# First attention chunk in more steps, a fifth exp buffer, weight loads on another queue, and a different filler pace

## Chip, cores and metric

The kernel runs on one core of one Trainium2 chip. The metric is device time in microseconds (us) of one execution; the median of several runs is quoted. All runs below are of the state that the measurement calls fast. The *granted clock* is the share of TensorE's full clock that the chip allowed, 1.00 at most.

## The reference

Two layers, each of attention and an MLP, with a residual and a layer norm (without gain) ahead of both. Everything is bfloat16.

```python
x = A_x                                  # [1, 2048, 512]
for _ in range(2):
    x = x + attention(layernorm(x), A_wqkv, A_wo)   # 32 heads of 16 columns
    x = x + relu(layernorm(x) @ B_w1) @ B_w2        # 512 -> 1792 -> 512
# attention: softmax(q k^T / 4) v per head, then @ wo
```

The exponentials are 2 layers x 32 heads x 2048 x 2048 elements, and they set the pace.

## The kernel before

A Python scheduler emits the whole program slot by slot. A **slot** is three blocks of scores (each 128 keys x 512 queries of one head) in three PSUM banks, and one ScalarE instruction that exponentiates them. In some slots ("short") the third block goes to a polynomial on VectorE, two such blocks making a **pair**. All other TensorE work, the **filler** (projections, MLP, transposes for layer norm), is put between the slots, and has one PSUM bank, `ps_f`, that VectorE must empty each time. Keys come in 16 row blocks, heads in four groups `T`, queries in four chunks `j`. While chunk 0 of layer 0 runs, the keys and values of the other chunks are still being made, so its runs are cut in two, with partial sums kept between:

```python
for l in range(2):
    early = range(TPC if l == 0 else NKB - TPC)      # TPC = 4, NKB = 16
    late = range(len(early), NKB)
    sums = acc0 if l == 0 else acc
    for T in range(4):
        add_run(l, 0, T, early, store=sums)
    for T in range(4):
        add_run(l, 0, T, late, load=sums)
    # ... cut: the other chunks
```

The order in which the filler for it is queued, and its pace in matmuls per slot:

```python
for j in range(1, NQS):
    # ... cut: layer norm of chunk j
    work.append(k_group(0, j, 0))
    work.extend(ln_groups(tag, xnT[j], 0, TPC, []))
    work.append(k_group(0, 0, j))
    work.extend(v_group(0, kb) for kb in range(j * TPC, (j + 1) * TPC))
for T in range(1, 4):
    work.extend(k_group(0, T, j) for j in range(1, NQS))

pace = (
    3.0 if first["short"] and not first["l"] else max(todo / max(rest + (AHEAD if first['l'] and first['j'] < NQS - 1 else -6.0), 6.0), 0.5)
)
```

If a slot needs something that is not made yet, the scheduler emits all that it depends on at once (`run_until`). The weight blocks of the MLP are loaded four ahead, from GpSimd's queue, which also holds the broadcast of the softmax sums:

```python
def load_w1(n):
    # ... cut
    nc.gpsimd.dma_start(out=w1buf[n % NW1][:], in_=B_w1[...])

def recip():                                        # softmax normalisation
    nc.vector.reciprocal(out=c, in_=c)
    nc.sync.dma_start(out=sums, in_=c)              # u<-c
    nc.gpsimd.dma_start(out=r[:, 0:width], in_=...) # r<-u, waits for u<-c
```

The matmuls of values with exponentials ("value matmuls") follow one or two slots later, and polynomial pairs are allowed from a certain point on:

```python
while len(pend) > held and len(musts) == copies:
    emit_pv()
# ... cut
elif len(pairs) < 2 and ("k", mine["l"], 0 if mine["l"] else 3, NQS - 1) in made:
```

The softmax here doesn't subtract the row's maximum and nothing guards it: scores larger than these inputs give would overflow.

## Time and profile before

| | before |
|---|---|
| median of three runs | 1783.71 us |
| span of the profiled run | 1781.0 us |
| ScalarE busy | 97% |
| full / short slots | 1071 / 294 |
| first and last exponential start | 16.9 / 1749.7 us |
| mean granted TensorE clock | 0.994 |

The lines are in the prediction.

### The profile page before, as it was taken

The page shows a single profiled execution, that of the slowest core. Times are in us where ns is not written, and L with a number is a line of the kernel's source. Part 1 is how long each engine was busy: PE and PEld are TensorE (multiplying, and loading weights), DVE is VectorE, ACT ScalarE, POOL GpSimd, SP SyncE. Part 2 cuts the span into 40 slices and gives each one's busy share as a digit, 9 for nine tenths or more (in the row PEclk, how much of TensorE's full clock was granted, in tenths as well). Part 3 has the DMA queues.
Part 4 walks back from the last instruction along what each step waited for, and adds up shares of the span by engine and source line. Part 5 has one row for each costly group of instructions (what it writes and reads, how often), then busy time and mean ns, then how long its engine had stood idle before and what let it go on. Part 6 is the DMA issues. An engine that isn't in the chain of part 4 may idle for free.

```text
span 1781.0 us, 35078 instructions
## 1 busy us (share of the span) xinstructions
PE 1643.0 (92%) x15322; PEld 517.8 (29%) x15322; DVE 1349.6 (76%) x2051; ACT 1724.1 (97%) x1386; POOL 149.4 (8%) x231
## 2 busy tenths in 40 slices
PE   8898889999999999999999998999999999999988
PEld 2222222222222222222222222222222222444444
DVE  7438778899899888898732244988888888898784
ACT  7979999999999999999999999999999999999994
POOL 1000000110001000110002000011000110002013
PEclk9989999999999999999999999999999999999999
DMA  4000100110011000110001002101100110102112
GB/s 148 1 7 14 19 15 10 40 26 13 9 22 38 16 13 14 23 40 14 9 9 39 1 3 37 19 17 37 25 20 11 28 35 19 23 14 47 26 31 66
DMA packets 50457, 44.54 MB, mean 25 GB/s; under 512 B 34304, under 2 KB 42240, under 8 KB 50304
## 3 DMA queue, kind: packets, MB, share of 16 engines
q0 software_dynamic: 23296, 33.15, 8.4%
q1 hardware_dynamic: 25664, 7.85, 1.8%
q8 instruction: 119, 1.95, 0.5%
q10 hardware_dynamic: 1344, 1.31, 0.2%
q14 instruction: 34, 0.28, 0.1%
HBM read 22.54 MB, written 2.10 MB: 14 GB/s over the span
## 4 chain that ended last, share of the span: by engine, by line
ACT 87%; PE 8%; DVE 3%; issue 2%; DMA 1%; POOL 0%; POOLq 0%
ACT e L1119 87%; PE ps_s L1110 2%; PE ps_f L403 2%; PE ps_o L806 2%; PE ps_s L1182 1%; DMA w<-in_B_w_dram 0%; DMA c<-u 0%; DVE di L852 0%; DVE dy L883 0%; DVE vaug L552 0%; DVE stats L432 0%; DVE de L883 0%; PE ps_f L1182 0%; PE ps_s L951 0%; DMA x<-in_A_x_dram 0%
## 5 line engine op out<-in xcount | busy, mean ns | idle before, releaser
L1119 ACT ACTIVATE e<-ps_s 128x1536 bf16<-128x1536 f32 (+1 forms) x1366 | 1713.7, 1472 | 20.1 <-PE ps_s L1110 19.3
L1110 PE MATMUL ps_s<-q,ktp 32*128 32x512 bf16 (+1 forms) x8114 | 769.0, 358 | 100.6 <-ACT e L1119 88.5
L806 PE MATMUL ps_o<-e,vaug 128*32 128x512 bf16 (+1 forms) x4270 | 429.5, 364 | 11.7 <-DVE u L744 6.2
L1110 PEld LDWEIGHTS <-ktp 32*128 32x128 bf16 x8114 | 235.8, 92 | 625.5 <-issue 523.0
L852 DVE TENSOR_SCALAR di<-ps_s 128x512 int32<-128x512 f32 x294 | 202.0, 687 | 94.8 <-PE ps_s L1110 92.7
L806 PEld LDWEIGHTS <-vaug 128*32 128x32 bf16 x5284 | 140.5, 94 | 295.3 <-issue 274.1
L883 DVE SCALAR_TENSOR_TENSOR dy<-dm 128x1024 f32<-128x1024 f32 x147 | 179.7, 1222 | 3.9
L883 DVE SCALAR_TENSOR_TENSOR dy<-dy,dm 128x1024 f32<-128x1024 f32 x147 | 178.6, 1215 | 2.7
L883 DVE SCALAR_TENSOR_TENSOR de<-dy,di 128x1024 bf16<-128x1024 f32 x147 | 178.2, 1212 | 1.8
L767 POOL DMA_DIRECT2D r<-u x70 | 51.0, 729 | 1260.6 <-DMA u<-c 373.7
L403 PE MATMUL ps_f<-xn2T,w 128*128 128x512 bf16 (+1 forms) x448 | 129.2, 374 | 5.1 <-DMA w<-in_B_w_dram 2.7
L601 POOL DMA_DIRECT2D w<-in_B_w_dram x126 | 96.2, 764 | 361.7 <-PE ps_f L403 340.8
L403 PE MATMUL ps_f<-w,ht 128*128 128x512 bf16 x392 | 117.8, 384 | 0.0
L616 DVE TENSOR_SCALAR ht<-ps_f 128x512 bf16<-128x512 f32 x105 | 72.2, 687 | 56.5 <-PE ps_f L403 56.2
L806 PE MATMUL ps_o<-de,vaug 128*32 128x512 bf16 (+1 forms) x676 | 104.7, 357 | 0.9
L877 DVE TENSOR_SCALAR dm<-di 128x1024 int32<-128x1024 int32 x147 | 103.2, 702 | 1.2
L877 DVE TENSOR_SCALAR di<-di 128x1024 int32<-128x1024 int32 x147 | 102.1, 695 | 2.2
L403 PE MATMUL ps_f<-xnT,wqkv 128*128 128x512 bf16 (+1 forms) x296 | 88.2, 376 | 2.8 <-DVE ktp L524 1.1
L403 PE MATMUL ps_f<-wo,ot 128*128 128x512 bf16 x240 | 74.0, 385 | 1.1 <-DVE x L587 1.1
L564 DVE TENSOR_SCALAR q<-ps_f,qmask 128x512 bf16<-128x512 f32 (+1 forms) x86 | 56.7, 692 | 15.0 <-PE ps_f L403 14.7
L757 DVE SCALAR_TENSOR_TENSOR ot<-u,mask,r 128x512 bf16<-128x512 f32 (+2 forms) x74 | 49.6, 671 | 23.8 <-DMA r<-u 23.6
L806 PE MATMUL ps_o<-di,vaug 128*32 128x512 bf16 (+1 forms) x338 | 66.1, 365 | 0.3 <-DVE di L877 0.3
(85 smaller groups left out, 561.9 us busy)
## 6 DMA issues: line engine op xcount, KB each, us to landing
w<-in_B_w_dram POOLq DMA_DIRECT2D x126, 128.0 KB, 2.6
r<-u POOLq DMA_DIRECT2D x56, 256.0 KB, 7.1
out_dram<-x SPq DMA_DIRECT2D x16, 128.0 KB
x<-in_A_x_dram SPq DMA_DIRECT2D x14, 128.0 KB
w<-in_B_w_dram SPq DMA_DIRECT2D x1, 1792.0 KB
r<-u POOLq DMA_DIRECT2D x14, 128.0 KB, 4.5
wqkv<-in_A_wqkv_dram ACTq DMA_DIRECT2D x2, 512.0 KB
c<-u SPq DMA_DIRECT2D x56, 8.0 KB
```

The source lines that it names most:

```text
L403: nc.tensor.matmul(out, lhsT, rhs, start=i % k == 0, stop=i % k == k - 1)
L564: return nc.vector.tensor_scalar(out=qbuf[n % 2][e][:, 0:w], in0=b, scalar1=qmask[e][:, 0:1], scalar2=None, op0=ALU.mult,)
L601: nc.gpsimd.dma_start(out=w1buf[n % NW1][:], in_=B_w1[:, ft * P : (ft + 1) * P].rearrange("(c p) f -> p c f", p=P),)
L616: nc.vector.tensor_scalar(out=htp[ft // 2][:, ft % 2 : ft % 2 + number, a : a + w], in0=b.rearrange("p (f q) -> p f q", f=number), scalar1 ...
L757: nc.vector.scalar_tensor_tensor(out=ot[t][:, at_column + a : at_column + a + w], in0=u[:, a : a + w], scalar=mask[e][:, 0:1], in1=r[:, a ...
L767: nc.gpsimd.dma_start(out=r[:, 0:width], in_=bass.AP(tensor=sums.tensor, offset=sums.offset, ap=[list(sums.ap[0]), [0, 32], [1, width]],),)
L806: nc.tensor.matmul(ps_o[32 * g : 32 * g + 32, 0 : sg["w"]], vaug[sg["l"]][kb][:, 4 * sg["T"] + g, 2 * e : 2 * e + 32], rhs, start=g not in ...
L852: first = nc.vector.tensor_scalar(out=di[:, half, :].bitcast(I32), in0=src, scalar1=EXP_BIAS, scalar2=0.0, op0=ALU.add, op1=ALU.max,)
L877: nc.vector.tensor_scalar(out=out[:].bitcast(I32), in0=di[:].bitcast(I32), scalar1=keep, scalar2=put, op0=ALU.bitwise_and, op1=ALU.bitwise_or,
L883: nc.vector.scalar_tensor_tensor(out=out[:], in0=x[:], scalar=c, in1=y[:], op0=ALU.add, op1=ALU.mult)
L1110: nc.tensor.matmul(b[:, a : a + sg["w"]], kt[32 * g : 32 * g + 32, kc : kc + P], qbuf[sg["n"] % 2][sg["e"]][32 * g : 32 * g + 32, 0 : sg[" ...
L1119: ex = nc.scalar.activation(out=eb[:, 0 : place[m]], in_=b[:, 0 : place[m]], func=ACTF.Exp, scale=1.0 / (LOG2E * UNIT),)
```

## The change

Its intent is to keep ScalarE fed: smaller steps in the first chunk, so that no run asks for keys before they are made; value matmuls held back when they would block the scores; weight loads in another queue; filler that need not be finished at a chunk's end.

```diff
-    NE = 4
+    NE = 5
-    AHEAD = 8.0
+    AHEAD = (8.0, 8.0)
+    LATE = 0.0
+    MID = 2
+    FIRST_K = {1: (1, 2, 3), 2: (), 3: ()}
...
-            nc.gpsimd.dma_start(
+            nc.sync.dma_start(
                 out=w1buf[n % NW1][:],
...
+        if l == 0:
+            steps = [(range(4), 0, TPC), (range(MID), TPC, 2 * TPC)]
+            steps += [(range(MID), 2 * TPC, NKB), (range(MID, 4), TPC, NKB)]
+        else:
+            steps = [(range(4), 0, NKB - TPC), (range(4), NKB - TPC, NKB)]
+        for Ts, a, b in steps:
+            for T in Ts:
+                sums = acc if l else acc0
+                add_run(l, 0, T, range(a, b), load=a and sums, store=b < NKB and sums)
...
-                nc.vector.tensor_copy(out=sg["store"], in_=ps_o[:])
+                if sg["load"] is not None:
+                    nc.vector.tensor_add(out=sg["store"], in0=sg["load"], in1=ps_o[:])
+                else:
+                    nc.vector.tensor_copy(out=sg["store"], in_=ps_o[:])
...
-        work.append(k_group(0, j, 0))
+        work.extend(k_group(0, T, 0) for T in FIRST_K[j])
...
+        if j == 1:
+            work.extend(k_group(0, T, 1) for T in range(1, MID))
     for T in range(1, 4):
-        work.extend(k_group(0, T, j) for j in range(1, NQS))
+        work.extend(k_group(0, T, j) for j in range(2 if T < MID else 1, NQS))
...
-   pace: rest + (AHEAD if first['l'] and first['j'] < NQS - 1 else -6.0)
+   pace: rest + (0.0 if first["j"] == NQS - 1 and not first["l"] else AHEAD[first["l"]] if first["j"] < NQS - 1 else -6.0)
...
         while len(pend) > held and len(musts) == copies:
+            start = pe_start("v", at([("po",)], "pe") if ("po",) in made else 0.0)
+            if len(pend) < NE - 1 and start + LATE > exp_end[no] - PE_TO_ACT - 2 * MM - SWITCH:
+                break
             emit_pv()
```

(The two pace lines are cut out of the long expression shown above; cuts are marked by "...".)

More of the change, by code (lines that the diff above doesn't have):

```diff
@@ L694, in add_run @@
                     "l": l, "j": j, "t": 2 * T + e, "e": e, "T": T, "kbs": kbs, "n": n,
-                    "load": load and load[2 * T + e], "store": store and store[2 * T + e],
+                    "load": load[2 * T + e] if load else None,
+                    "store": store[2 * T + e] if store else None,
                     "w": columns(l, j)[2], "begun": set(), "left": 4 * len(kbs), "short": bool(load or store), "early": bool(store), "busy": len(kbs) == TPC,
@@ L700 @@
     for l in range(2):
-        early = range(TPC if l == 0 else NKB - TPC)
-        late = range(len(early), NKB)
-        sums = acc0 if l == 0 else acc
-        for T in range(4):
-            add_run(l, 0, T, early, store=sums)
-        for T in range(4):
-            add_run(l, 0, T, late, load=sums)
+        if l == 0:
[7 more added lines that the diff above has]
+                add_run(l, 0, T, range(a, b), load=a and sums, store=b < NKB and sums)
         for j in range(1, NQS + l):
@@ L1084 @@
         pace = (
-            3.0 if first["short"] and not first["l"] else max(todo / max(rest + (AHEAD if first['l'] and first['j'] < NQS - 1 else -6.0), 6.0), 0.5)
+            3.0 if first["short"] and not first["l"] else max(todo / max(rest + (0.0 if first["j"] == NQS - 1 and not first["l"] else AHEAD[first["l"]] if first["j"] < NQS - 1 else -6.0), 6.0), 0.5)
         )
```

## The prediction

> **What bounds the kernel now.** I read the page first: busy time by engine, then the costliest groups. ScalarE is busy for 97% of the span, nearly all of it in one instruction, the exponential at L1119 (1366 times). A slot, below, is one such instruction with the score matmuls that feed it. I then took that line by shape, because its mean mixes full slots (1536 columns) with short ones (1024 columns, the third block being given to a VectorE polynomial).
>
> ```profile
> PE 1643.0 (92%) x15322; PEld 517.8 (29%) x15322; DVE 1349.6 (76%) x2051; ACT 1724.1 (97%) x1386; POOL 149.4 (8%) x231
> L1119 ACT ACTIVATE e<-ps_s 128x1536 bf16<-128x1536 f32 (+1 forms) x1366 | 1713.7, 1472 | 20.1 <-PE ps_s L1110 19.3
> ...
> L1119 ACT ACTIVATE e<-ps_s 128x1536 bf16<-128x1536 f32 x1071 | 1499.5, 1567 | 17.7 <-PE ps_s L1110 17.0
> L1119 ACT ACTIVATE e<-ps_s 128x1024 bf16<-128x1024 f32 x294 | 331.7, 1129 | 2.4 <-PE ps_s L1110 2.3
> ```
>
> Durations overlap (1366 x 1472 ns is more than the busy 1713.7), so the price of a slot is the distance between starts. The view of the one line in a stretch gives first and last start. From 878.8 to 1070.0 us there are 144 slots, 142 full and 2 short: 191.2 us for 141 full and 2 short intervals. From 299.5 to 499.3 us there are 162 intervals, about 120 full and 42 short. The two together give **1.343 us for a full slot and about 0.926 for a short one**. At these rates 1071 full and 294 short intervals are 1438 + 272 = 1710 us. The first exponential starts at 16.9 and the last at 1749.7, 1733 us apart. So **some 22 us are lost** between them, and the head (17 us) and the tail after the last exponential (31 us) lie outside.
>
> Where are the 22? The same sum, stretch by stretch: start to 106.8 us, 59 full intervals are 79.2 us but took 89.9, **10.7 lost**. 829.0 to 874.8: 1.7 lost. 1068.6 to 1149.8: 2.8. 1499.5 to 1599.4: 0.9. 1718.5 to 1749.7: 18 full and 2 short are 26.0 but took 31.2, **5.2 lost**. The others lose nothing that I can resolve. The waits of ScalarE say the same of the large ones; first the stretch 0 to 120 us, then 1725 to 1740:
>
> ```profile
> ACT e L1119 <- PE ps_s L1110: 10.5, 6, 5.9
> ```
> ```profile
> ACT e L1119 <- PE ps_s L1110: 4.7, 3, 3.4
> ```
>
> The timeline of the first loss shows the cause. The scheduler had put off chunk 2's normalised rows and its K and V until slot 52 could not go on without them:
>
> ```profile
> 87.83 0.38 PE L471 MATMUL ps_f<-ident,xn 128*128 128x128 bf16 x4 [0.46 <-DVE vaug L552]
> ...
> 89.62 0.58 PE L471 MATMUL ps_f<-ident,xn 128*128 128x128 bf16 x4 [0.51 <-DVE xnT L507]
> ...
> 91.82 1.86 PE L403 MATMUL ps_f<-xnT,wqkv 128*128 128x512 bf16 x4 [0.52 <-DVE xnT L507]
> ...
> 95.12 1.45 ACT L1119 ACTIVATE e<-ps_s 128x1536 bf16<-128x1536 f32 x1 [5.91 <-PE ps_s L1110]
> ```
>
> Four groups of transposes each wait for VectorE to empty the one PSUM bank, then come K and four V groups in a row, and ScalarE starves. The table by stretch adds that the granted clock was 0.50 from 90 to 98 us: four K matmuls took 1.86 us there, against 1.02 for the four V matmuls at 103.49 us.
>
> The second loss is in the timeline at the end:
>
> ```profile
> 1726.38 0.68 POOL L767 DMA_DIRECT2D r<-u  x1 [11.61 <-DMA u<-c]
> ...
> 1727.05 3.38 POOL L601 DMA_DIRECT2D w<-in_B_w_dram  x4
> ...
> 1732.26 1.89 PE L403 MATMUL ps_f<-xn2T,w 128*128 128x256 bf16 x8 [2.65 <-DMA w<-in_B_w_dram]
> ...
> 1734.76 1.45 ACT L1119 ACTIVATE e<-ps_s 128x1536 bf16<-128x1536 f32 x1 [3.39 <-PE ps_s L1110]
> ```
>
> GpSimd's queue is in order. Four loads of MLP weights stand behind the broadcast r<-u, which waits for the DMA u<-c; TensorE then waits for weights whose buffers had been free since about 1724.8.
>
> **What the Trainium skill says.** *Perfetto Trace Analysis*, Identifying the Most-Contended Engine: occupancy is a fair measure for Scalar and Vector, not for matmul busy time; so 97% ScalarE is the bound and 92% TensorE is not proof of one. The trace agrees: the stretch from 878.8 ran at the full slot rate with TensorE about 90% busy. *ScalarE: Activation LUTs*, Rules for kernel authors: about 0.3 us plus 0.83 ns an element; here 512 columns are worth 1.343 - 0.926 = 0.417 us, 0.81 ns each, which agrees. *TensorE: Matmul & The Clock Gate*, Part 1: after a window of some 3.4 us with little activity the clock falls to half. The trace agrees: half rate follows 3 us of lone transposes and, in the tail, the 2.65 us wait. *DMA: Bandwidth & Descriptors*, Issuing engines are not separate DMA queues: another issuing engine saves only the sequencer's time. Here an issue takes 0.75 us on GpSimd and 0.54 on SyncE; but the trace shows a second effect, what stands ahead in the queue.
>
> **The change, part by part.** I compared the order of both built programs, counting TensorE's matmuls between neighbouring slots.
>
> (1) *More steps in the first chunk.* Runs of head groups 0 and 1 take row blocks 4 to 7 before they need the rest. That inserts 2 groups x 2 head parities x 4 blocks x 4 heads = 64 blocks, 21 slots, 28 us, before chunk 2 is needed. It costs four more partial sums (4 adds in place on VectorE at about 0.69 us) and two more runs (10 for 8), each with a q group of 4 matmuls and 2 masked copies. VectorE is 27 to 50% busy from 60 to 120 us, so this is hidden. In the new order no slot of the first hundred carries more than 4 transposes or 4 projection matmuls; the 16 transposes and 4 matmuls of slot 52 are gone. At 2 to 4 such matmuls of 0.22 us per slot, with scores and values at about 0.6 us, TensorE stays at or just under 1.343. I take 2 of the 10.7 us as remaining, for short waits on the single filler bank: **-8.7 us**. The lull that lowered the clock goes too, and is in this number.
>
> (2) *Price of it.* The polynomial may start only when the last K group of the chunk is made. The first short slot moves from number 80 to 90, and the program has 145 pairs, not 147: 290 short and 1075 full slots, not 294 and 1071. 4 x 0.417 = **+1.7 us**.
>
> (3) *Weight loads on the sync queue.* In the new order the four late loads stand right behind u<-c, which was issued at 1724.08, not behind r<-u. They can go at about 1724.8 (two) and 1727.6 (two), when their buffers are free. With 2.6 us to landing, the page's median for these loads, the first two are there by about 1728.5 (1724.8, two issues of 0.54, 2.6), and TensorE asks at about 1729.6. The wait and the half clock after it go; I leave 1 of 5.2 us: **-4.2 us**. The 126 issues x 0.75 us that GpSimd no longer makes were not on the path. At the start the loads move behind the other inputs; the head is a chain of VectorE normalisation steps, so nothing is gained there.
>
> (4) *Filler past chunk ends.* In layer 0 the filler had to be done six slots before a chunk's end; now it may run past it. Only the last chunk (829 to 875) loses anything now, 1.7 us, with TensorE packed; the new order has 33, 16, 36 projection matmuls in slots 640 to 699, not 32, 24, 22, so the pack is thinned: **-1.0 us**.
>
> (5) *Five exp buffers and the held value matmuls.* A value matmul that would wait for VectorE to empty the accumulator no longer stands ahead of the next scores. The loss at 1070 to 1150 has such a wait (0.96 us at 1140.3), but the new order is nearly the same there: **-0.5 us**.
>
> Sum: -8.7 + 1.7 - 4.2 - 1.0 - 0.5 = **-12.7 us**; 1783.7 - 12.7 = 1771.0.
>
> **Rivals.** *The loss in the first chunk only moves.* The work to be made there is the same, with two runs more, and TensorE is nearly full over 90 slots instead of 52: every filler group waits for the one bank, 0.5 us or more each. If half of the gain is lost so, the time is 1775. For it: ScalarE lost some already at 57 to 61 us. Against: the waits seen there are under 1 us, and no clump is left. *The sync queue becomes the place to wait.* Loads wait for TensorE, and c<-u and u<-c now stand behind them, so normalisation comes late. For it: DMA c<-u is on the path near 1098 us. Against: there are no weight loads near there, and three buffers of 26 us segments give slack elsewhere. It would cost 1 to 3 us, so 1773. *All losses go:* 22 us less and 1.7 more for the pairs, about 1763; no step above removes the last of each loss. *VectorE gains from a quiet GpSimd:* it is not the bound; nothing.
>
> **Range and chances.** The middle is 1771; the moved loss and the sync queue pull up by up to 6, more thorough removal pulls down by up to 5: 1766 to 1777. A change of 2% is 35.7 us, more than all that is lost, so faster is nearly impossible; a slowdown by as much would need a new wait of 48 us.
>
> **What would show it.** ScalarE's waits in the first 120 us near 2 us, not 10.5, with a clock of 1.0 from 80 to 105; the last 30 slots without a wait on w, the w issues on SyncE; 290 short slots; 31 us still after the last exponential. It would be wrong if ScalarE's start distances rose in the steady stretches, if new waits of scores on the filler bank added up in the first chunk, or if normalisation's DMAs came late behind weight loads.

## The result

The changed kernel took 1769.88 us (four runs, 1769.66 to 1770.96), the kernel before 1784.02 (four runs, 1782.05 to 1784.73). A ratio, here and below, is the mean time of one kernel's fast runs over that of the other's of the same rounds, so not quite the ratio of the medians: **0.9924, interval 0.9907 to 0.9941**. That is within 2%, and inside the range.

The engines' busy times and the costliest group of the changed kernel, in the same form as before:

```profile
PE 1602.8 (91%) x15093; PEld 518.6 (29%) x15289; DVE 1340.4 (76%) x2045; ACT 1724.3 (97%) x1386; POOL 53.5 (3%) x105
...
L1131 ACT ACTIVATE e<-ps_s 128x1536 bf16<-128x1536 f32 (+1 forms) x1366 | 1713.9, 1481 | 5.9 <-PE ps_s L1122 5.1
```

ScalarE is as busy as before; only its idle time before an exponential has fallen, from 20.1 to 5.9 us. GpSimd lost the 126 load issues.

The waits of ScalarE from 0 to 120 us, where there were 10.5 us:

```profile
ACT e L1131 <- PE ps_s L1122: 0.4, 1, 0.4
```

From 1700 to 1745 us the exponential does not occur in that view at all. The table by stretch for 90 to 105 us, first of the kernel before, then of the changed one (columns: stretch, its length, busy us and instruction count of TensorE, its weight loads, VectorE, ScalarE and GpSimd, then the granted clock, DMA share and GB/s):

```profile
90.00:105.00 15.00, 13.26 (x69) 3.51 (x68) 4.06 (x7) 7.04 (x5) 0.00 (x0) 0.67 0.00 1
```
```profile
90.00:105.00 15.00, 13.37 (x115) 4.47 (x113) 6.74 (x12) 15.00 (x13) 0.00 (x0) 1.00 0.00 1
```

TensorE was equally "busy" in both, but at two thirds of the clock and with 69 matmuls instead of 115; ScalarE went from 7 to the full 15 us. Matmul busy time alone would have hidden the loss. And the end, where the weights were late, as a timeline of the changed kernel:

```profile
1716.07 0.54 SPq L776 DMA_DIRECT2D u<-c  x1
...
1716.66 19.68 SPq L604 DMA_DIRECT2D w<-in_B_w_dram  x14
...
1718.37 0.68 POOL L777 DMA_DIRECT2D r<-u  x1 [11.61 <-DMA u<-c]
...
1721.53 1.05 PE L406 MATMUL ps_f<-xn2T,w 128*128 128x256 bf16 x8
```

The loads go out right behind u<-c, 1.7 us before r<-u is issued (before, they came 0.7 us after it), and the eight matmuls that waited 2.65 us now start without a wait and at full clock.

From first to last exponential the changed kernel took 1718.6 us (17.9 to 1736.5), 14.2 us less than before. By the prediction's prices its 1075 full and 290 short slots are 1712.3 us, so some 6 us are lost where it was 22. Its head was 1.0 us and its tail 1.4 us longer in the profiled run. Both go with half clock: from 12 to 14 us the granted clock was 0.50 (the first eight projection matmuls took 2.72 us, not 1.89), and from 1748 to 1750 it was 0.52. In the second profiled run of the changed kernel (e9), without these spells, the head was 16.9 us again and the tail 31.0, and e10, with the loads in the old queue, had a head of 18.3 us with a clock of 0.66 from 10 to 15 us; so it is not the moved loads.

### The profile page after: what moved, and what is told of

It reads as the page before. It is cut to its first block, busy times and chain, and to the rows that moved or that the text cites. A ratio compares the mean times of both kernels' runs of the same rounds, so it can differ in the third digit from the quotient of the medians.

```text
span 1769.2 us, 34798 instructions
## 1 busy us (share of the span) xinstructions
PE 1602.8 (91%) x15093; PEld 518.6 (29%) x15289; DVE 1340.4 (76%) x2045; ACT 1724.3 (97%) x1386; POOL 53.5 (3%) x105
## 4 chain that ended last, share of the span: by engine, by line
ACT 80%; PE 7%; issue 2%; DVE 2%; DMA 0%; ACTq 0%
ACT e L1131 80%; PE ps_s L1122 3%; PE ps_o L816 2%; PE ps_f L406 1%; PE ps_s L1197 1%; DVE di L862 0%; DMA c<-u 0%; PE ps_f L1197 0%; DVE dy L893 0%; DVE q L567 0%; DVE u L754 0%; DVE de L893 0%; DVE u L752 0%; DVE x L647 0%; DVE dm L887 0%
## 5 line engine op out<-in xcount | busy, mean ns | idle before, releaser
L893 DVE SCALAR_TENSOR_TENSOR dy<-dm 128x1024 f32<-128x1024 f32 x145 | 177.2, 1222 | 3.5
L893 DVE SCALAR_TENSOR_TENSOR dy<-dy,dm 128x1024 f32<-128x1024 f32 x145 | 176.2, 1215 | 2.8
L893 DVE SCALAR_TENSOR_TENSOR de<-dy,di 128x1024 bf16<-128x1024 f32 x145 | 175.9, 1213 | 1.8
L406 PE MATMUL ps_f<-xn2T,w 128*128 128x512 bf16 (+1 forms) x390 | 114.0, 368 | 5.6 <-DVE ht L619 2.3
L406 PE MATMUL ps_f<-w,ht 128*128 128x512 bf16 x339 | 105.3, 384 | 4.2 <-issue 3.8
L406 PE MATMUL ps_f<-xnT,wqkv 128*128 128x512 bf16 (+1 forms) x266 | 81.3, 371 | 4.6 <-issue 1.4
L406 PE MATMUL ps_f<-wo,ot 128*128 128x512 bf16 x207 | 65.7, 384 | 2.7 <-issue 2.1
L767 DVE SCALAR_TENSOR_TENSOR ot<-u,mask,r 128x512 bf16<-128x512 f32 (+2 forms) x74 | 49.6, 671 | 14.3 <-DMA r<-u 14.2
L406 PEld LDWEIGHTS <-w 128*128 128x128 bf16 x448 | 33.2, 97 | 81.9 <-issue 73.0
```

The lines of the kernel that those rows point to most:

```text
L406: nc.tensor.matmul(out, lhsT, rhs, start=i % k == 0, stop=i % k == k - 1)
L767: nc.vector.scalar_tensor_tensor(out=ot[t][:, at_column + a : at_column + a + w], in0=u[:, a : a + w], scalar=mask[e][:, 0:1], in1=r[:, a ...
L893: nc.vector.scalar_tensor_tensor(out=out[:], in0=x[:], scalar=c, in1=y[:], op0=ALU.add, op1=ALU.mult)
```

## The experiments

Four kernels carry one part of the change each (e1 to e4), and three the whole but one part (e5, e10, e11). Four add something of mine (e6, e7, e8, e12), and e9 is the changed kernel again. Kernels of one call ran on one chip and shared the runs of the kernel before; e1 to e4 are one call, e5 to e8 the second, e9 to e12 the third. The second call ran on another chip than the other two. All results were correct.

| run | median us | ratio to before | interval |
|---|---|---|---|
| e1 sync queue alone | 1776.62 | 0.9967 | 0.9949 to 0.9985 |
| e2 steps alone | 1774.44 | 0.9954 | 0.9938 to 0.9970 |
| e3 pace alone | 1780.63 | 0.9986 | 0.9971 to 1.0001 |
| e4 hold alone | 1783.30 | 1.0005 | 0.9991 to 1.0019 |
| e5 all but hold | 1769.34 | 0.9926 | 0.9909 to 0.9943 |
| e6 no hold, earlier polynomial | 1770.04 | 0.9930 | 0.9914 to 0.9947 |
| e7 and pairs 20 slots apart | 1769.37 | 0.9933 | 0.9916 to 0.9949 |
| e8 and pairs 10 slots apart | 1776.59 | 0.9971 | 0.9955 to 0.9987 |
| e9 the changed kernel again | 1769.36 | 0.9939 | 0.9924 to 0.9954 |
| e10 all but sync queue | 1774.96 | 0.9965 | 0.9950 to 0.9979 |
| e11 all but pace | 1770.94 | 0.9944 | 0.9930 to 0.9958 |
| e12 hold, earlier polynomial | 1768.56 | 0.9929 | 0.9915 to 0.9943 |

### e1: the loads on the sync queue, alone

```diff
-            nc.gpsimd.dma_start(      # in load_w1
+            nc.sync.dma_start(
```

> The kernel before with the MLP weight loads moved to the sync queue and nothing else. Theory (the loads stood in GpSimd's queue behind the broadcast r<-u): the wait of 2.65 us on w near the end and the half clock after it go, ScalarE's waits between 1710 and 1745 us fall from 4.7 to under 1 us, and the time falls by 4 to 5 us, to about 1779. The 10.5 us in the first chunk stay. Rival (c<-u and u<-c now wait behind weight loads): the normalisation comes late and eats the gain, so the time falls by less than 2 us. Rival (VectorE is faster with a quiet GpSimd): the time falls by more than 6 us and the steady stretches get faster.

The mean fell by 0.33%, 5.9 us, more than the 4 to 5 expected, but the interval runs from 2.7 to 9.1. The trace is clearer: from 1700 to 1745 us the exponential no longer waits, where it had waited 4.7 us, and the loss of that stretch against the slot sum is 5.2 us before and 0.1 here. In the first chunk 9.5 us of waits stay. So the loads' being in GpSimd's queue was the cause. No run separates their place behind r<-u from SyncE's shorter issue (0.37 us for 0.75), but the trace before does in part: the first late load, issued 0.7 us after r<-u, needed 5.2 us to land, where the median is 2.6. Issued at 1724.8 us, when its buffer was free, it would by that median have landed at about 1727.4 even from GpSimd (an estimate), and TensorE asked at 1729.6. The first rival needs c<-u and u<-c to delay something; between 120 and 800 us ScalarE's waits are 0.2 us as before. The second falls too: the steady stretches are as long as before, and VectorE's polynomial steps keep their durations (1222, 1215 and 1212 ns before, 1223, 1216 and 1213 in e1).

### e2: the steps of the first chunk, alone

```diff
-    early, late (two passes over four head groups)
+    steps = [(range(4), 0, TPC), (range(MID), TPC, 2 * TPC)]
+    steps += [(range(MID), 2 * TPC, NKB), (range(MID, 4), TPC, NKB)]
     # with FIRST_K, the order of K groups and the store that adds, as in the change
```

> The kernel before with only the first chunk's attention in more steps and the new order of its K groups; 290 short slots instead of 294. Theory: the clump of 16 transposes and 4 matmuls before slot 53 is the whole loss of the first chunk, so ScalarE's waits up to 120 us fall from 10.5 to about 1 us, the clock stays at 1.0 between 85 and 105 us, and with 1.7 us paid for the four longer slots the time falls by 7 to 9 us, to about 1776. Rival (the loss only moves, the same work meeting the one filler bank over more slots): waits of 4 us or more remain there and the time falls by 3 to 5 us.

The mean fell by 0.46%, 8.2 us. ScalarE's waits up to 120 us are 0.4 us, and the clock is 1.00 in every 5 us from 85 to 105. The rival is out: nothing of the loss came back in that chunk, and from 120 to 800 us the waits are 0.2 us as before. The wait at the end is there as it was, which shows that the parts act in different places:

```profile
1717.99 3.38 POOL L604 DMA_DIRECT2D w<-in_B_w_dram  x4
...
1723.16 1.89 PE L406 MATMUL ps_f<-xn2T,w 128*128 128x256 bf16 x8 [2.61 <-DMA w<-in_B_w_dram]
...
1725.65 1.45 ACT L1131 ACTIVATE e<-ps_s 128x1536 bf16<-128x1536 f32 x1 [3.34 <-PE ps_s L1122]
```

### e3: the filler's pace, alone

```diff
-   rest + (AHEAD if first['l'] and first['j'] < NQS - 1 else -6.0)
+   rest + (0.0 if first["j"] == NQS - 1 and not first["l"] else AHEAD[first["l"]] if first["j"] < NQS - 1 else -6.0)
```

> The kernel before with only the filler's pace changed (in layer 0 it may run past a chunk's end). Theory: only the last chunk of layer 0 (829 to 875 us) loses anything there, 1.7 us, and that goes: the time falls by 1 to 2 us. Rival: the thinning is hidden and nothing changes (within 0.5 us), or work left over at chunk ends collides with the next chunk and it gets slower by 1 us or more.

The ratio 0.9986 has 1 in its interval, so the time does not decide it. The trace has the predicted effect (the loss from 819 to 869 us is 0.5 us instead of 1.7) and a cost that I had not thought of: ScalarE's waits from 120 to 800 us went from 0.2 to 1.1 us. Between these two the gain is too small to be measured alone.

### e4: five buffers and the hold, alone

```diff
-    NE = 4
+    NE = 5
         while len(pend) > held and len(musts) == copies:
+            start = pe_start(...)
+            if len(pend) < NE - 1 and start + LATE > exp_end[no] - PE_TO_ACT - 2 * MM - SWITCH:
+                break
```

> The kernel before with only the fifth exp buffer and the held value matmuls. Theory: the scores no longer stand behind a value matmul that waits for VectorE to empty the accumulator, so the loss of 2.8 us at 1069 to 1150 us shrinks by about 1 us, and the time falls by 0.5 to 1.5 us. Rival: nothing changes (within 0.5 us), because the waits are elsewhere.

The rival: no gain (1.0005). The theory's stretch from 1060 to 1160 us has 2.3 us of waits against 2.0, and new waits appeared elsewhere. ScalarE's waits from 120 to 800 us, 0.2 us before, are here:

```profile
ACT e L1119 <- PE ps_s L1110: 2.3, 5, 0.6
```

### e5: the change without the hold

```diff
-    NE = 5
+    NE = 4
-            start = ...   # the three lines of the hold
```

> The changed kernel with four exp buffers and without the held value matmuls; the rest of the change stays. Theory after the single parts (alone, the held value matmuls raised ScalarE's waits between 120 and 800 us from 0.2 to 2.3 us and took 0.6 from the loss at 1060 to 1145): the part is worth nothing, so the waits between 120 and 800 us fall from 2.8 us to under 1, those at 1060 to 1160 rise from 0.8 to about 1.5, and the time is that of the changed kernel within 2 us (about 1769), rather lower. Rival (the parts need each other: the tighter first chunk is only free of waits because value matmuls are held): waits of 2 us or more come back before 120 us and the time is 2 us or more higher.

At 1769.34 the part is not missed. No wait came back in the first 120 us (0.4 us), so the steps do not need it. From 120 to 800 us the waits fell to 1.8, not under 1. From 1060 to 1160 us they were 3.7 us, more than the 1.5 expected; but that execution had the clock at 0.50 from 1100 to 1105 us.

The traces of e1 to e6, e9 to e12 and the two kernels can tell what the hold does in that stretch. TensorE pauses there in two places of the kernel before: the scores wait for `q` from VectorE, and a value matmul waits for VectorE's copy of the accumulator, the wait that the hold is for.

```profile
1103.79 0.80 PE L1110 MATMUL ps_s<-q,ktp 32*128 32x512 bf16 x7 [0.92 <-DVE q L564]
...
1140.30 0.38 PE L806 MATMUL ps_o<-e,vaug 128*32 128x512 bf16 x1 [0.96 <-DVE u L744]
```

ScalarE alone, first before, then in e1, where TensorE has the same second pause at 1139.19:

```profile
1104.63 37.87 ACT L1119 ACTIVATE e<-ps_s 128x1024 bf16<-128x1024 f32 x31 [0.86 <-PE ps_s L1110]
1143.10 1.45 ACT L1119 ACTIVATE e<-ps_s 128x1536 bf16<-128x1536 f32 x1 [0.60 <-PE ps_s L1110]
1145.13 15.97 ACT L1119 ACTIVATE e<-ps_s 128x1024 bf16<-128x1024 f32 x13 [0.59 <-PE ps_s L1110]
```
```profile
1103.52 57.67 ACT L1119 ACTIVATE e<-ps_s 128x1024 bf16<-128x1024 f32 x47 [0.87 <-PE ps_s L1110]
```

The first pause is in all twelve traces, and ScalarE waits after it. The second is in all six without the hold and in none of the six with it, so the hold does what it was made for; but in e1 ScalarE did not notice it. The rest of the waits follows the clock. Without a spell of half clock in this stretch ScalarE waits 0.8 to 0.9 us (the changed kernel, e1, e12), with one spell 1.7 to 2.3 (eight traces, with and without the hold), with two 3.7 (e5: from 1098.3 and from 1135.8 us).

### A reading across runs: the granted clock

The runs of one kernel differ by up to 10 us. Set beside its mean granted clock, each run falls nearly on a line (the rows for 0.991, 0.993, 0.995 and 0.996, which only the kernel before has, are left out):

| mean clock | kernel before, us | changed kernel, us |
|---|---|---|
| 0.992 | 1785.00 to 1785.97 | none |
| 0.994 | 1782.75 to 1784.26 | none |
| 0.997 | 1779.03 to 1779.33 | none |
| 0.998 | 1779.26 | 1770.96 to 1771.58 |
| 0.999 | 1776.44 | 1769.17 to 1770.04 |
| 1.000 | none | 1768.69 |

A straight line through the 34 runs before with a listed clock falls by 1.24 us for each 0.001, and one through the 9 runs of the changed kernel by 1.40. Half clock appears in spells after a stretch in which TensorE did little. In the profiled runs each spell that ended before the run did lasted 3.41, 6.83 or 10.24 us, and within a run the spells begin whole multiples of 3.41 us apart (before: 89.65, 1140.95 and 1731.46 us, 308 and 173 such steps). Whether a lull is hit differs from run to run: the half clock near 1732 us after the wait for weights was there in the trace before, in e2, e4 and e10, and absent in e3, where the same wait cost 2.4 us in all instead of 4.7. With the clump and the late weights gone, there are fewer lulls to be hit. The mean clock rose from 0.9949 (34 runs) to 0.9988 (9 runs); at 1.24 us for 0.001 that is about 5 of the 12 us between the two means, 1782.1 and 1770.0. This is an estimate from a correlation, not an experiment on the clock. Two cautions for what follows. The listed clock is rounded to 0.001, and so much is worth 1.24 to 1.40 us: a difference of 1 us between a few runs at equal listed clock is a hint, not a result. And a change that removes lulls raises the clock itself, so a comparison at equal clock leaves out part of what it won.

### e9: the changed kernel again

(No edit.)

> The changed kernel again, on the chip of this call, because the runs so far show that a kernel's time follows its mean granted clock (about 1.3 us for 0.001). Theory: the clock of the changed kernel is not fixed at the 0.998 to 0.999 of its first four runs; it varies as for the others, and the time with it, 1769.7 us at 0.999 and about 1.3 us more per 0.001. Rival (the change makes the clock steady): all six runs at 0.998 or more and within 1.5 us of 1770.

Half of my theory fell: the clock of the five runs was 0.998 to 1.000, and all lay between 1768.69 and 1771.58 (the rival's 1.5 us was missed by one run, by 0.08). For these nine runs the change did make the time steadier. The other half held: the time followed the clock, 1768.69 at 1.000 and 1771.22 and 1771.58 at 0.998. The ratio, 0.9939, is nearer to 1 than the first, because the kernel before ran at 1780.36 in this call.

### e10: the change without the sync queue

```diff
-            nc.sync.dma_start(
+            nc.gpsimd.dma_start(
```

> The changed kernel with the MLP weight loads back on GpSimd's queue. Theory (the parts act in different places and add): the wait of about 2.5 to 3.4 us near the end is back, with or without a spell of half clock after it, and nothing else: 3 to 6 us slower than the changed kernel on this chip, about 1774. Rival (another part removes the same wait): within 1.5 us of the changed kernel.

The mean was 1774.6 against 1770.0 for e9, 4.6 us slower, and ScalarE waits 3.5 us near the end again. The rival is out, and 4.6 is the better number for this part, since the runs of these two spread by 2.6 and 2.9 us and those of the kernel before by 8.6 in this call. Part of the 4.6 is half clock: the mean clock was 0.9972 in e10 and 0.9988 in e9.

### e11: the change without the pace

```diff
-   rest + (0.0 if first["j"] == NQS - 1 and not first["l"] else AHEAD[first["l"]] if ...)
+   rest + (AHEAD[1] if first['l'] and first['j'] < NQS - 1 else -6.0)
```

> The changed kernel with the old filler pace. Theory after the single part (at equal clock, 0.997, it stood at 1779.4 against 1779.3 for the kernel before): the thinner filler takes 1 us of waits from 819 to 869 us and gives about as much back between 120 and 800, so at equal clock the time is that of the changed kernel within 1 us. Rival (it is worth the 1 us or more of the prediction): at equal clock more than 1 us slower.

The mean was 1770.8, 0.8 us above e9; at a clock of 0.999 the four runs are 1770.16 to 1771.02 and the five of the changed kernel 1769.17 to 1770.04. The loss from 819 to 869 us is back at 2.0 us (0.2 with the change). The two profiled runs, with one like spell of half clock before the end each (from 1097.6 and 1097.8 us), have spans of 1767.6 (e9) and 1768.4 us. So beside the other parts the pace seems worth about 1 us, on the border between theory and rival; it does not show in the ratios, and the times alone do not settle it.

### e6 and e12: the polynomial earlier in the first chunk

The change paid for its steps with two pairs. Both kernels give them back; e6 is without the hold, e12 with it.

```diff
-   ("k", mine["l"], 0 if mine["l"] else 3, NQS - 1) in made
+   ("k", mine["l"], 0 if mine["l"] else 1, NQS - 1) in made
```

> The changed kernel without the hold, and with the polynomial allowed in the first chunk once K group 1 of the last row block is made, rather than group 3: 294 short slots again, the first at number 76, not 90. Theory (the two lost pairs cost 4 x 0.417 us): 1.7 us less than the changed kernel without the hold, about 1767. Rival (VectorE and the filler bank are too busy there, so the short slots only turn into waits): ScalarE's waits before 170 us rise by 1.5 us or more and the time stays.

> The changed kernel with its hold, and the polynomial allowed in the first chunk once K group 1 of the last row block is made: 294 short slots. Theory: at equal clock 4 x 0.417 = 1.7 us faster than the changed kernel, near 1768.1 at 0.999. Rival: the earlier short slots turn into waits before 170 us and nothing is gained.

e12 has the lowest median of all, 1768.56, but its interval overlaps that of e9. At a clock of 0.999 its four runs (1768.41 to 1768.78) lie 1.0 us below the mean of the changed kernel's five (1769.6), and e6's two (1767.28 and 1767.42) as far below e5's two (1768.30 and 1768.41). So the two pairs seem worth about 1 us rather than 1.7, within the rounding of the clock. In e12, ScalarE's waits from 120 to 800 us are 3.9 where they were 2.8, but that run had a spell of half clock from 518.8 us that the changed kernel's did not. Neither gain is one that the ratios resolve. By median e6 shows nothing, since its clock ran from 0.994 to 0.999.

### e7 and e8: pairs where they were forbidden

In layer 1's first chunk the polynomial waits for the last K group, some 160 slots. Here it may start a pair 20 or 10 slots after the last one.

```diff
+   (... in made or (mine["l"] and no >= last_pair[0] + 20))   # e8: 10
...
                 pair_at = no + 2 if half == 0 else None
+                last_pair[0] = no
```

> As the one before, and in layer 1's first chunk, where the polynomial was forbidden for some 160 slots, one pair may begin at least 20 slots after the last: 302 short slots. Theory (ScalarE is the only bound there, with VectorE about 35% busy): 8 more short slots x 0.417 = 3.3 us less, about 1764. Rival (TensorE, 90% busy there, is the next bound, since a pair's values take three passes): the 190 us stretch keeps its length and the waits take the gain.

> The same with a distance of 10 slots: 310 short slots, but two groups of 8 filler matmuls are now forced at once near slots 831 and 841. Theory: another 8 x 0.417 = 3.3 us less in the stretch, 1 to 2 us given back at the forced groups, so about 1762. Rival (TensorE becomes the bound): no better than the distance of 20, with new waits of 3 us or more between 870 and 1150 us.

Neither theory held in full. e7 gained in its stretch, 146 slots in 189.6 us where the changed kernel had 143 in 190.2, but gave it back in the next: ScalarE's waits from 1060 to 1160 us are 6.3 us. In the timeline TensorE waits for VectorE to add the accumulator to the sums kept before, that addition stands behind a product with r, and the product waits for a DMA:

```profile
1104.34 0.75 DVE L767 SCALAR_TENSOR_TENSOR ot<-u,mask,r 128x512 bf16<-128x512 f32 x1 [4.22 <-DMA r<-u]
...
1106.34 0.59 PE L816 MATMUL ps_o<-e,vaug 128*32 128x512 bf16 x1 [3.93 <-DVE u L752]
...
1107.52 1.45 ACT L1133 ACTIVATE e<-ps_s 128x1536 bf16<-128x1536 f32 x1 [3.72 <-PE ps_s L1124]
```

e8 is clearly worse, with 14.3 us of waits there, and 3.0 from 900 to 1060 us:

```profile
ACT e L1133 <- PE ps_s L1124: 14.3, 8, 3.7
```

The rival had the result right (new waits after 1060 us eat the gain), and only part of the cause: e7's largest wait, 3.72 of 6.3 us, is the normalisation chain and not TensorE's rate. Of e8's three largest, two (3.66 us before 1071.3 and 3.43 before 1090.6) follow a q group and a K group made one after the other, TensorE standing 1.50 us for VectorE's `q` between them; the third (3.02 before 1113.4) is the chain again. What the five smaller ones follow I did not separate.

## Why the prediction was right

**The bound and the loss.** The sum by start distances was the step that carried everything: ScalarE bound, 22 us lost between the exponentials, most of it in two places. The changed kernel has the same busy ScalarE and 14.2 us less between first and last exponential.

**(1) and (2), steps, predicted -8.7 and +1.7.** The mechanism is shown by e2. The size of the first term was off: I left 2 us for waits on the filler bank, and there are none (61 intervals at 1.343 us are 81.9, and 17.9 to 99.6 us took 81.7). So it is -10.7 in the profiled pair, half clock included. One reading of the timeline was off: half clock did not follow 3 us of lone transposes, it began at 89.65 us, 1.8 us after the first of them (87.83). The price of the lost pairs, +1.7, is 290 short slots as counted; e6 and e12, which give the pairs back, seem to have won about 1 us.

**(3), sync queue, predicted -4.2.** Shown by e1 and e10: 5.9 us with a wide interval, and 4.6. I had left 1 us of the stretch's 5.2; 0.1 is left. Where I assumed 0.54 us for an issue on SyncE, the number of another transfer, these loads took 0.37. Two things in the trace before were not in the account: the first late load also took 5.2 us to land, twice the median of 2.6 that the sum used, and half clock began at 1731.46 us, inside the wait and 1.9 us after TensorE's last matmul.

**(4), pace, predicted -1.0.** The trace has it (1.7 us lost before, 0.2 after), e3 did not resolve it, and e11 suggests about 1 us. Not seen in advance was the cost of about 1 us in the steady stretches.

**(5), hold, predicted -0.5.** This step failed. Alone it won nothing and added about 2 us of waits in the steady stretches; without it the rest is as fast (e5). Its two runs at a listed 0.999 are about 1 us below the changed kernel's (1768.30 and 1768.41 against 1769.6), but on another chip and within the rounding of the clock. The pause of 0.96 us that the prediction named goes with the hold, as its mechanism says, but it was not what ScalarE lost there: at full clock that is the wait for `q`, which the hold does not touch, and the rest is half clock that came or did not come (0.9 us in e1, which has no hold; 0.8 and 1.7 in two runs of the changed kernel). Whether the hold makes the clock steadier stays open. The mean is 0.9988 with it over nine runs and 0.9978 over five without (e5), 0.9990 in e12 and 0.9970 in e6, but both without it ran on the other chip; a way would be there, since spells began after either pause and the hold takes one away.

**The rivals.** "The loss only moves" fell with e2. "The sync queue becomes the place to wait" fell with e1 and e10. "VectorE gains from a quiet GpSimd" fell with its unchanged durations.

**What the sum did not have.** The single parts by ratio make -5.9 - 8.2 - 2.5 + 0.9 = -15.7 us; the whole measured -13.5 (0.9924) and -10.9 (0.9939), which intervals of about 3 us either way on each number allow. That the middle was met within 1.1 us is in part luck: the profiled pair shows 2.0 us more won by (1) and 0.9 by (3), and against them 2.6 us of new waits from 120 to 800 us that no term has. The prediction took one trace as if its half clock were the kernel's own. It was a usual run of a spread from 1776 to 1787 us, so the middle was safe, but a base at a clock of 0.999 instead of 0.994 would have shown a loss some 6 us smaller (an estimate, by the line above).

## What to carry to other kernels

When one engine bounds a kernel, price its unit by the distance between starts in a clean stretch, subtract that from every stretch, and look for the cause of each remainder; here two remainders held most of what was to be won. In a queue that works in order, ask what stands ahead of a transfer, not only which engine issues it. When a change is worth a few us and the clock of the runs varies, compare runs of equal granted clock before believing an ordering, unless the change itself removes the pauses that lower it; and leave out a part, not only add it, before calling it useful.

## What the Trainium skill lacked or had wrong

- *ScalarE: Activation LUTs*, Rules for kernel authors: its budget gives the mean duration of one exponential (0.3 us plus 1536 x 0.83 ns is 1.57 us; 1.567 measured), but back to back the starts are 1.343 us apart, 0.22 less. The budget's row says nothing of overlap; an overlap of about 93 ns stands further up on the page (What ACT_TABLE_LOAD costs), and it fits only the exponentials that follow a wait, which take 1.45 us (0.11 over the distance).
- *TensorE: Matmul & The Clock Gate*, Part 1: the half clock after a lull is as described (0.50 here), but it took less of a lull than the idle window of about 3.4 us in the page's table: in the 3.41 us before 1731.46 TensorE was busy for 1.56 us by the records, before 1140.95 for 2.21, with a longest pause of 0.96. What is missing is its effect on comparing kernels: 0.001 of mean clock went with 1.24 to 1.40 us, and runs of the kernel before spread from 1776.44 to 1787.18 us.
- *DMA: Bandwidth & Descriptors*, Issuing engines are not separate DMA queues: it has another issuing engine save only the sequencer's time. Here moving 126 loads won 4.6 to 5.9 us, because a waiting transfer stood ahead of them in the old queue.
- On no page that I read: an issue of the same 128 KB load took 0.75 us on GpSimd and 0.37 us (median) on SyncE, and by the packet counts of the two pages a load was 48 packets from GpSimd and 528 from SyncE (126 loads: 6048 fewer in one queue, 66528 more in the other).
